# An attention and feed-forward layer: norms deferred by urgency, projections held until their rows are loaded, first norms at once, last tile in quarters

## The chip, the cores and the metric

One core of one Trainium2 chip runs the whole kernel. The time is the device time of one execution in microseconds (us). Medians are given with the number of executions behind them. A kernel's runs also carry the mean clock that was granted to TensorE (1.000 is full speed): in the runs quoted here the mean clock of one kernel differs from run to run by a few thousandths, and the time with it (the kernel before, on one chip: 918.45 us at 0.996, 917.06 at 0.998, 916.01 at 1.000). Profiled spans are some 1.7 us shorter than the times of the same executions; spans are compared with spans, and times with times.

## The reference, cut to what matters

```python
h   = x + attention(layernorm(x)) @ wo            # S=2048, D=1024, bf16
out = h + (silu(layernorm(h) @ w1) * (layernorm(h) @ w3)) @ w2   # F=3584
# attention: 32 heads of 32; 4 segments of 512 rows, one after the other.
# In a segment: softmax attention inside the segment, plus phi(q) @ M / (phi(q) @ z)
# from a memory M, z summed over earlier segments, mixed by sigmoid(beta).
```

## The kernel before

The program does not write instructions in order. It builds a graph of operations. Each has an engine, an estimated duration and a class (a lower class is more urgent), and a list scheduler fixes, at build time, the order of each engine and the semaphore waits. So a changed class or dependence moves instructions everywhere, and a dependence added to the graph is a wait in the finished kernel only where the order does not satisfy it anyway.

The kernel lets its matmuls write to one PSUM tensor of 128x4096 fp32, which its code counts as eight banks of 128x512. While attention runs, four hold scores, bank 4 and bank 5 numerators and denominators, and only banks 6 and 7 are free for all dense matmuls. A dense group (the eight matmuls of one accumulation, and the operation that evacuates the bank) takes one of the two. It is `safe`: its first matmul also takes over the write-after-read dependences of its later operations, so that a group doesn't occupy a bank and then wait.

```python
    # Graph.op: every operation joins the graph here
            if group.safe and group.ops:
                head = group.ops[0]
                for d, raw in list(o.deps.items()):
                    if not raw and d.seq < head.seq:
                        self.dep(head, d, raw=False)
# ... cut ...
    def dense_group(self, late=False):
        g = Group([(6,), (7,)],
                  ("att", [(4,), (5,), (0,), (1,), (2,), (3,)]) if late else None, True)
        return g
# ... cut ...
    def ln(self, k, src, dst, cls):               # statistics at cls - 1, L716 and L718
        # ... cut ...
        self.dve_op(lambda e: e.tensor_scalar(dst, src, mean, rs, op0=ALU.subtract,
                                              op1=ALU.mult), 540.0, [src, mean, rs], [dst], cls,
                    port=True)                    # the norm itself, L725
# ... cut ...
    def wo_stage(self, s):                        # output projection of segment s
        oT = self.oT[s % 2]
        for i in range(4):
            t = 4 * s + i
            h, hn = self.h[t % 3], self.hn[0]     # 3 buffers of rows, 1 of normed rows
            self.g.dma(h[:, :], self.x2d[t * 128:(t + 1) * 128, :], cls=2)
            for half in range(2):
                gr = self.dense_group(s >= 2)
                self.mms(gr, [(lambda gr: self.bank(gr), oT[:, c, i * 128:(i + 1) * 128],
                               self.wo[:, c, half * 512:(half + 1) * 512], c == 0, c == 7, 512)
                              for c in range(8)], 5 if s < 2 else 7)
                hs = h[:, half * 512:(half + 1) * 512]
                self.g.op("dve", dve_ns(512), lambda e, gr, hs=hs: [e.tensor_tensor(
                    hs, hs, self.bank(gr), op=ALU.add)], reads=[hs], writes=[hs], cls=1,
                    group=gr)                     # the residual add, L993
            self.g.dma(self.hd[t * 128:(t + 1) * 128, :], h[:, :], cls=3)
            self.ln(16 + t, h[:, :], hn[:, :], 4)
            self.g.dma_t(self.hnT[s][:, :, i * 128:(i + 1) * 128], hn[:, :], 2)
```

The residual add reads rows `h` that a DMA loads. That dependence is a true read-after-write one, so the safe group doesn't pass it to its first matmul: the group may take its bank before its rows are there.

The softmax here doesn't subtract the row's maximum and nothing guards it: scores larger than these inputs give would overflow.

Of the kernel before, what the change touches and what calls it, by code (L numbers as in the profile page):

```python
# [8 lines left out]
ALU = mybir.AluOpType  # L9
# [60 lines left out]
class Graph:  # L70
# [90 lines left out]
    def op(self, engs, cost, emit, reads=(), writes=(), cls=5, deps=(), group=None,  # L161
           kind=None, gate=None, port=False):
        if isinstance(engs, str):
            engs = (engs,)
        if not isinstance(cost, dict):
            cost = {e: cost for e in engs}
        o = Op(engs, cost, emit, cls, len(self.ops))
        o.kind = kind
        o.gate = gate
        o.port = port  # L170
        if gate is not None:
            self.phase_left[gate] = self.phase_left.get(gate, 0) + 1
        for ap in reads:
            self._touch(o, ap, False)
        for ap in writes:
            self._touch(o, ap, True)
        for d in deps:
            self.dep(o, d)
        o.group = group
        for group in (group.parts if isinstance(group, Both) else (group,) if group else ()):  # L180
            for prev in group.ops:
                if prev.engs != o.engs or o.engs != ("pe",):
                    self.dep(o, prev)
            if group.ops and o.engs == ("pe",):
                self.dep(o, group.ops[-1])
            o.first = not group.ops
            if group.safe and group.ops:
                head = group.ops[0]
                for d, raw in list(o.deps.items()):
                    if not raw and d.seq < head.seq:  # L190
                        self.dep(head, d, raw=False)
            group.ops.append(o)
            group.open += 1
        self.ops.append(o)
        return o
# [259 lines left out]
def act_ns(n, ptr=0):  # L455
    return 185.0 + n * 0.834 + 93.0 * ptr


def dve_ns(n, mode=1):
    return 150.0 + n / (0.96 * mode)  # L460
# [10 lines left out]
class Kernel:  # L471
# [219 lines left out]
    def ln_act(self, k, src, dst):  # L691

        sm, nm, sq = (self.lnst[:, k, i:i + 1] for i in range(3))
        junk = self.oT[0][:, 0:2, :].rearrange("p a b -> p (a b)")
        G = self.g
        G.op("act", act_ns(1024), lambda e, gr: [e.activation(junk, src, AF.Copy, accum_out=sm)],
             reads=[src], writes=[junk, sm], cls=1)
        self.act(nm, sm, AF.Copy, 190.0, cls=1, scale=-1.0 / 1024)
        G.op("act", act_ns(1024, 1), lambda e, gr: [e.activation(
            junk, src, AF.Square, bias=nm, accum_out=sq)], reads=[src, nm], writes=[junk, sq],  # L700
            cls=1)
        ve, rs = self.lnve[:, k:k + 1], self.rstd[:, k:k + 1]
        mh = self.mhalf[:, :]
        self.pool_op(lambda e: e.tensor_scalar(ve, sq, 1.0 / 1024, self.EPS, op0=ALU.mult,
                                               op1=ALU.add), 1, [sq], [ve], 0)
        self.pool_op(lambda e: e.tensor_tensor(rs, ve, mh, op=ALU.pow), 190, [ve, mh], [rs], 0)
        self.dve_op(lambda e: e.tensor_scalar(dst, src, nm, rs, op0=ALU.add, op1=ALU.mult),
                    540.0, [src, nm, rs], [dst], 2, port=True)

    def ln(self, k, src, dst, cls):  # L710

        st = self.lnst[:, k, :]
        mv = self.lnmv[:, k, :]
        for c in range(2):
            a, b = self.lnst[:, k, 6 * c:6 * c + 6], src[:, c * 512:(c + 1) * 512]
            self.dve_op(lambda e, a=a, b=b: e.bn_stats(a, b), 630.0, [b], [a], cls - 1)  # L716
        st2 = self.lnst[:, k, :].rearrange("p (a b) -> p a b", a=2)
        self.dve_op(lambda e: e.bn_aggr(mv, st2), 200.0, [st2], [mv], cls - 1)  # L718
        ve, rs = self.lnve[:, k:k + 1], self.rstd[:, k:k + 1]
        var, mean = self.lnmv[:, k, 1:2], self.lnmv[:, k, 0:1]  # L720
        mh = self.mhalf[:, :]
        self.pool_op(lambda e: e.tensor_scalar(ve, var, self.EPS, None, op0=ALU.add), 1,
                     [var], [ve], 0)
        self.pool_op(lambda e: e.tensor_tensor(rs, ve, mh, op=ALU.pow), 190, [ve, mh], [rs], 0)
        self.dve_op(lambda e: e.tensor_scalar(dst, src, mean, rs, op0=ALU.subtract,  # L725
                                              op1=ALU.mult), 540.0, [src, mean, rs], [dst], cls,
                    port=True)

    def ln1(self, s):
        for i in range(4):  # L730
            t = 4 * s + i
            x = self.xs[t % 4][:, :]
            self.g.dma(x, self.x2d[t * 128:(t + 1) * 128, :], cls=0 if s == 0 else 2)
            if t == 1:
                self.ln_act(t, x, x)
            else:
                self.ln(t, x, x, 2 if s == 0 else 5)
            if s:
                self.g.dma_t(self.xnT[s][:, :, i * 128:(i + 1) * 128], x, 3)
                continue  # L740
            gr = Group([(6,), (7,), (4,), (5,)], safe=True)
            self.transposes(gr, [(c * 128, self.xs[t % 4][:, c * 128:(c + 1) * 128])
                                 for c in range(8)], 2 if s == 0 else 4)
            out = self.xnT[s][:, :, i * 128:(i + 1) * 128]
            self.evac(gr, out, 1024, lambda b: b.rearrange("p (k n) -> p k n", k=8), cls=1,
                      bf=True)
# [234 lines left out]
    def wo_stage(self, s):  # L981
# [3 lines that stand above are left out]
            h, hn = self.h[t % 3], self.hn[0]  # L985
# [8 lines that stand above are left out]
                    hs, hs, self.bank(gr), op=ALU.add)], reads=[hs], writes=[hs], cls=1,  # L994
                    group=gr)
            self.g.dma(self.hd[t * 128:(t + 1) * 128, :], h[:, :], cls=3)
            self.ln(16 + t, h[:, :], hn[:, :], 4)
            self.g.dma_t(self.hnT[s][:, :, i * 128:(i + 1) * 128], hn[:, :], 2)

    def ffn_up(self, blk, ch):  # L1000
# [30 lines left out]
    def ffn_down(self, blk):  # L1031
        if blk == 0:
            for i in range(7):
                self.g.dma(self.w2[i][:, :, :], self.B_w2[i * 512:(i + 1) * 512, :].rearrange(
                    "(j p) n -> p j n", p=128), cls=5)
        for i in range(8):
            t = 8 * blk + i
            hr = self.hr[t % 3]
            self.g.dma(hr[:, :], self.hd[t * 128:(t + 1) * 128, :], cls=3)
            for half in range(2):  # L1040
                gr = self.dense_group(True)
                self.mms(gr, [(lambda gr: self.bank(gr), self.hm[fc][:, i * 128:(i + 1) * 128],
                               self.w2[fc // 4][:, fc % 4, half * 512:(half + 1) * 512],
                               fc == 0, fc == 27, 512) for fc in range(28)], 8,
                         eager=True)
                ob = self.ob[self.n_ob % 8][:, :]
                self.n_ob += 1
                hs = hr[:, half * 512:(half + 1) * 512]
                self.g.op("dve", dve_ns(512), lambda e, gr, hs=hs, ob=ob: [e.tensor_tensor(  # L1049
                    ob, hs, self.bank(gr), op=ALU.add)], reads=[hs], writes=[ob], cls=1,  # L1050
                    group=gr)
                self.g.dma(self.out2d[t * 128:(t + 1) * 128, half * 512:(half + 1) * 512], ob,
                           cls=1)

    def run(self):
        self.ps = self.es.enter_context(self.nc.psum_tensor("ps", [128, 4096], F32))
# [83 lines left out]
```

## Time and profile before

| | before |
|---|---|
| time, median of 4 runs beside the changed kernel | 917.87 us (916.94 to 918.2) |
| profiled span | 916.2 us, mean clock 0.996 |
| TensorE | 99% busy |
| TensorE idle in the first 332 us | 9.3 us |
| TensorE idle from 332 us to the last matmul | 0 |
| half clock | 6.83 us, from 150.9 us |

The prediction shows the lines of this profile that carry its argument. One view is added here, TensorE's waits: what it waited for, the total in us, how often, and the longest one.

```profile
PE ps L610 <- DVE xs L725: 2.4, 1, 2.4
PE ps L871 <- ACT et L884: 2.0, 5, 0.8
PE ps L598 <- DVE R0b L970: 1.5, 1, 1.5
...
PE ps L598 <- DVE h L993: 0.9, 3, 0.6
```

The first is the wait for the first norm at start-up. The third and part of the second and fourth are one place, at 148 to 152 us, which the prediction takes apart. L598 is the line of every dense matmul, L610 of the transposes, L871 of the scores, L939 of attention's numerators and denominators, L884 of the exponential. The products with the memory are `pq,zsel` and `pq,Mbf`; the second needs bank 4. 128\*128, 32\*128 and 128\*32 are the tiling modes, as the profile prints them with each matmul. A change of mode has no line of its own. The 0.10 us that the prediction gives it is an estimate from this trace: eight dense matmuls start 0.216 us apart from 25.95 us on, a score group in another mode starts at 27.77 and the next dense matmul at 28.10, so a group of some 0.21 us takes 0.33.

The trace's record of the granted clock changes at 4.17, 150.94, 157.77 and 915.53 us, the last time to half after the last matmul. From the first change these are 43, 45 and 267 times 3.413 us. A stretch of 3.41 us between two such multiples is called a window below. In the two windows at half clock, dense matmuls that follow each other start 0.427 us apart, as from 155.03 to 157.16, and at full clock 0.216.

### The profile page before, as it was taken

To read this page: it belongs to the slowest core of one execution; us is meant where nothing else is said; L and a number is where in the kernel's file an instruction comes from. 1 tells how busy PE (TensorE), PEld (TensorE's weight loads), DVE (VectorE), ACT (ScalarE), POOL (GpSimd) and SP (SyncE) were. 2 spreads that over 40 slices of the span, in tenths; PEclk is the share of its full clock that TensorE was granted. 3 is DMA by queue.
4 is the path that set the end of the run, shared out by engine and by line. 5 is a ranking of instruction groups with operands and counts; after the bars stand their busy time and mean duration, and the time that the engine had idled before them with its cause. 6 is when DMAs were issued, how large, how long until landed. Compare 5 with 4: busy or idle time off the path is not lost.

```text
span 916.2 us, 12998 instructions
## 1 busy us (share of the span) xinstructions
PE 904.0 (99%) x5472; PEld 404.1 (44%) x5472; DVE 432.8 (47%) x735; ACT 297.7 (32%) x316; POOL 176.2 (19%) x274
## 2 busy tenths in 40 slices
PE   8999998999999999999999999999999999999998
PEld 5444443444444444444444444444444444444443
DVE  3867877877856764634634311211343334331111
ACT  5878865877677611111111100000111111110000
POOL 2545655456553420100100000000000000000000
PEclk9999998999999999999999999999999999999999
DMA  9957655443531355833733121012133212301110
GB/s 311 248 166 214 156 138 116 127 126 112 141 119 41 90 207 158 187 101 93 174 102 92 47 70 47 14 38 80 53 98 92 64 52 69 93 24 40 35 41 29
DMA packets 145241, 96.26 MB, mean 105 GB/s; under 512 B 45344, under 2 KB 132384, under 8 KB 145184
## 3 DMA queue, kind: packets, MB, share of 16 engines
q1 hardware_dynamic: 145184, 95.45, 37.9%
q8 instruction: 43, 0.70, 0.3%
q14 instruction: 14, 0.11, 0.1%
HBM read 76.55 MB, written 8.39 MB: 93 GB/s over the span
## 4 chain that ended last, share of the span: by engine, by line
PE 96%; ACT 1%; DVE 1%; DMA 0%; issue 0%; SPq 0%; DVEq 0%
PE ps L598 89%; PE ps L939 4%; PE ps L871 3%; ACT et L884 1%; DMA xs<-in_A_x_dram 0%; DVE lnst L716 0%; PE ps L610 0%; DVE h L993 0%; DVE hn L725 0%; SPq L203 0%; DVE T L950 0%; DVE R0b L965 0%; DVE R0b L970 0%; DVE qT L622 0%; DVE xnT L622 0%
## 5 line engine op out<-in xcount | busy, mean ns | idle before, releaser
L598 PE MATMUL ps<-hnT,w1b 128*128 128x512 bf16 x896 | 223.2, 379 | 0.0
L598 PE MATMUL ps<-hnT,w3b 128*128 128x512 bf16 x896 | 222.3, 379 | 0.0
L1019 ACT ACTIVATE sg<-ps 128x512 bf16<-128x512 f32 x112 | 66.9, 597 | 442.6 <-PE ps L598 439.9
L598 PE MATMUL ps<-w2b,hm 128*128 128x512 bf16 x896 | 196.3, 379 | 0.0
L1022 DVE SCALAR_TENSOR_TENSOR t<-sg,ps 128x512 bf16<-128x512 bf16 x112 | 76.9, 687 | 210.6 <-ACT sg L1019 210.6
L884 ACT ACTIVATE et<-ps 128x2048 bf16<-128x2048 f32 x80 | 149.9, 1874 | 34.2 <-PE ps L871 17.9
L598 PEld LDWEIGHTS ps<-w2b,hm 128*128 128x128 bf16 x896 | 87.7, 98 | 105.7
L598 PEld LDWEIGHTS ps<-hnT,w3b 128*128 128x128 bf16 x896 | 87.3, 98 | 106.0 <-issue 1.2
L598 PEld LDWEIGHTS ps<-hnT,w1b 128*128 128x128 bf16 x896 | 87.0, 98 | 106.3 <-issue 6.4
L889 POOL TENSOR_SCALAR_AFFINE_SELECT et<-et 128x512 bf16<-128x512 bf16 x128 | 88.7, 710 | 118.6 <-ACT et L884 118.3
L1027 DVE SCALAR_TENSOR_TENSOR hm<-t,ps 128x512 bf16<-128x512 bf16 x112 | 76.9, 687 | 37.6 <-PE ps L598 34.5
L1049 DVE TENSOR_TENSOR ob<-hr,ps 128x512 bf16<-128x512 bf16 x32 | 22.0, 687 | 143.4 <-PE ps L598 143.4
L598 PE MATMUL ps<-hnT,wp 128*128 128x512 bf16 x256 | 63.5, 390 | 0.9 <-DVE h L993 0.6
L598 PE MATMUL ps<-xnT,wp 128*128 128x512 bf16 (+1 forms) x288 | 60.2, 356 | 0.3 <-DVE xnT L622 0.3
L598 PE MATMUL ps<-wo,oT 128*128 128x512 bf16 x256 | 59.5, 380 | 0.3 <-DVE h L993 0.3
L950 DVE STREAM_TRANSPOSE T<-ps 128x512 f32<-128x512 f32 x32 | 22.9, 717 | 37.4 <-PE ps L939 37.3
L598 PEld LDWEIGHTS ps<-xnT,wp 128*128 128x128 bf16 x288 | 26.5, 98 | 27.1 <-issue 4.2
L598 PEld LDWEIGHTS ps<-hnT,wp 128*128 128x128 bf16 x256 | 23.7, 100 | 31.8 <-issue 7.2
L598 PEld LDWEIGHTS ps<-wo,oT 128*128 128x128 bf16 x256 | 24.0, 98 | 30.7 <-issue 2.2
L976 POOL TENSOR_TENSOR Nm<-Nm,R1b 128x512 f32<-128x512 f32 x24 | 30.4, 1268 | 32.6 <-DVE R1b L965 32.5
L871 PE MATMUL ps<-qT,kT 32*128 32x128 bf16 (+3 forms) x512 | 31.9, 302 | 2.2 <-ACT et L884 2.0
L598 PE MATMUL ps<-wp,hnT 128*128 128x512 bf16 x128 | 30.8, 380 | 0.0
(85 smaller groups left out, 592.6 us busy)
## 6 DMA issues: line engine op xcount, KB each, us to landing
w1b<-in_B_w_dram SPq DMA_DIRECT2D x28, 512.0 KB, 3.9
w3b<-in_B_w_dram SPq DMA_DIRECT2D x28, 512.0 KB, 4.7
wp<-in_A_wk_dram SPq DMA_DIRECT2D x8, 1024.0 KB, 5.6
wp<-in_A_wv_dram SPq DMA_DIRECT2D x8, 1024.0 KB, 5.3
wp<-in_A_wq_dram SPq DMA_DIRECT2D x7, 1024.0 KB, 5.7
w2b<-in_B_w_dram SPq DMA_DIRECT2D x7, 1024.0 KB, 8.6
xs<-in_A_x_dram SPq DMA_DIRECT2D x16, 256.0 KB, 5.8
h<-in_A_x_dram SPq DMA_DIRECT2D x16, 256.0 KB, 3.3
```

The source lines that it names most:

```text
L598: return [e.matmul(p[0](gr), p[1], p[2], start=p[3], stop=p[4]) for p in part]
L871: ins.append(e.matmul(self.bank(gr, j, 512 - 128 * kc, off), k[r, g, 128 * kc:128 * kc + 128], q[r, g, 128 * kc:512], start=True, stop=Tru ...
L884: return [e.activation(et[:, :, :], src, AF.Exp, scale=self.scale)]
L889: self.pool_op(lambda e, m=m: e.affine_select(m, m, pattern=[[0, 4], [1, 128]], compare_op=ALU.is_ge, fill=0.0, base=0, channel_multiplier ...
L939: ins.append(e.matmul(self.ps[r, b * 512 + 128 * kc:(b + 1) * 512], lhsT, pieces[kc][:, j, :], start=kc == 0 and (what == "n" or s == 0), ...
L950: G.op("dve", dve_ns(512), lambda e, gr: [e.transpose(T1, self.bank(gr))], writes=[T1], cls=0, group=gd)
L976: self.either(lambda e: e.tensor_tensor(Nm, Nm, R1, op=ALU.mult), 512, 2, [Nm, R1], [Nm], 2)
L1019: self.g.op("act", act_ns(512), lambda e, gr, sg=sg: [e.activation(sg, self.bank(gr), AF.Tanh, scale=0.5)], writes=[sg], cls=2, group=gg)
L1022: e.scalar_tensor_tensor(t1, sg, 1.0, self.bank(gr), op0=ALU.add, op1=ALU.mult)], reads=[sg], writes=[t1], cls=2,
L1027: e.scalar_tensor_tensor(dst, t1, 0.5, self.bank(gr), op0=ALU.mult, op1=ALU.mult)], reads=[t1], writes=[dst], cls=2,
L1049: self.g.op("dve", dve_ns(512), lambda e, gr, hs=hs, ob=ob: [e.tensor_tensor(ob, hs, self.bank(gr), op=ALU.add)], reads=[hs], writes=[ob], ...
```

## The change

Four edits, all of the order; apart from the last tile, which is cut differently, no instruction is added or removed by hand.

1. **Hold**: the first matmul of a dense group also takes over a dependence on a load, so a projection claims its bank only when its rows are there.
2. **Deferral**: the norms after the projection go from class 4 to 6, those of later segments from 5 to 5, 6 and 7, so that evacuations go ahead of them.
3. **First norms at once**: the norms of the first four tiles get class 0.
4. **Quarters**: the last output tile is computed in columns of 512, 256 and 256, so that the last evacuation and store are half as large.

```diff
-                    if not raw and d.seq < head.seq:
-                        self.dep(head, d, raw=False)
+                    if (not raw or d.kind == "dma") and d.seq < head.seq:
+                        self.dep(head, d, raw=raw)
@@ ln_act, the norm itself
-                    540.0, [src, nm, rs], [dst], 2, port=True)
+                    540.0, [src, nm, rs], [dst], 0, port=True)
@@ ln, the norm itself
-                                              op1=ALU.mult), 540.0, [src, mean, rs], [dst], cls,
-                    port=True)
+                                              op1=ALU.mult), 540.0, [src, mean, rs], [dst],
+                    0 if k < 4 else cls, port=True)
@@ ln1
-                self.ln(t, x, x, 2 if s == 0 else 5)
+                self.ln(t, x, x, 2 if s == 0 else 4 + s)
@@ wo_stage
-            self.ln(16 + t, h[:, :], hn[:, :], 4)
+            self.ln(16 + t, h[:, :], hn[:, :], 6)
@@ ffn_down
-            for half in range(2):
+            cols = [(0, 512), (512, 256), (768, 256)] if t == 15 else [(0, 512), (512, 512)]
+            for c0, n in cols:
                 gr = self.dense_group(True)
     ... cut: matmuls, add and store of columns c0 to c0 + n in place of half * 512 to ... + 512
```

More of the change, by code (lines that the diff above doesn't have):

```diff
@@ L1039, in ffn_down @@
             self.g.dma(hr[:, :], self.hd[t * 128:(t + 1) * 128, :], cls=3)
-            for half in range(2):
+            cols = [(0, 512), (512, 256), (768, 256)] if t == 15 else [(0, 512), (512, 512)]
+            for c0, n in cols:
                 gr = self.dense_group(True)
-                self.mms(gr, [(lambda gr: self.bank(gr), self.hm[fc][:, i * 128:(i + 1) * 128],
-                               self.w2[fc // 4][:, fc % 4, half * 512:(half + 1) * 512],
-                               fc == 0, fc == 27, 512) for fc in range(28)], 8,
-                         eager=True)
-                ob = self.ob[self.n_ob % 8][:, :]
+                self.mms(gr, [(lambda gr, n=n: self.bank(gr, 0, n),
+                               self.hm[fc][:, i * 128:(i + 1) * 128],
+                               self.w2[fc // 4][:, fc % 4, c0:c0 + n],
+                               fc == 0, fc == 27, n) for fc in range(28)], 8, eager=True)
+                ob = self.ob[self.n_ob % 8][:, 0:n]
                 self.n_ob += 1
-                hs = hr[:, half * 512:(half + 1) * 512]
-                self.g.op("dve", dve_ns(512), lambda e, gr, hs=hs, ob=ob: [e.tensor_tensor(
-                    ob, hs, self.bank(gr), op=ALU.add)], reads=[hs], writes=[ob], cls=1,
+                hs = hr[:, c0:c0 + n]
+                self.g.op("dve", dve_ns(n), lambda e, gr, hs=hs, ob=ob, n=n: [e.tensor_tensor(
+                    ob, hs, self.bank(gr, 0, n), op=ALU.add)], reads=[hs], writes=[ob], cls=1,
                     group=gr)
-                self.g.dma(self.out2d[t * 128:(t + 1) * 128, half * 512:(half + 1) * 512], ob,
-                           cls=1)
+                self.g.dma(self.out2d[t * 128:(t + 1) * 128, c0:c0 + n], ob, cls=1)
     def run(self):
```

## The prediction

> **What bounds the kernel now.** I read four views in this order: the page's busy shares, busy time by stretch, TensorE's order of time around each place where it waits, and the order of time of all engines at the worst of them. First the page and the stretches.
>
> ```profile
> PE 904.0 (99%) x5472; PEld 404.1 (44%) x5472; DVE 432.8 (47%) x735; ACT 297.7 (32%) x316; POOL 176.2 (19%) x274
> ...
> 0.00:332.00 332.00, 322.69 (x2780) 0.99 0.54 148
> 332.00:913.20 581.20, 581.20 (x2696) 1.00 0.29 81
> 913.20:916.20 3.00, 0.08 (x1) 0.89 0.13 44
> ```
>
> The reader is to see that TensorE is the bound and that most of the span is closed to this change. From 332 us on, 2696 matmuls take 581.2 us, 0.2156 us each, with no idle time: that is the feed-forward part, already a solid stream. Everything that a new order can win lies in the first 332 us (9.3 us shown idle, plus any slow clock) and in the 3 us after the last matmul. Two per cent would be 18.4 us, more than all of that together. So the answer "within 2%" is nearly settled before the change is read.
>
> Then the one bad place, in TensorE's order of time:
>
> ```profile
> 146.89 1.04 PE L598 MATMUL ps<-wo,oT 128*128 128x512 bf16 x4
> 147.79 0.39 PE L598 MATMUL ps<-pq,zsel 128*128 128x512 bf16 x1
> 148.94 0.40 PE L871 MATMUL ps<-qT,kT 32*128 32x256 bf16 x8 [0.77 <-ACT et L884]
> 150.81 0.52 PE L598 MATMUL ps<-pq,Mbf 128*128 128x512 bf16 x1 [1.47 <-DVE R0b L970]
> 151.32 0.61 PE L871 MATMUL ps<-qT,kT 32*128 32x512 bf16 x4
> ...
> 152.50 1.86 PE L598 MATMUL ps<-hnT,wp 128*128 128x512 bf16 x4 [0.56 <-DVE h L993]
> 154.16 1.07 PE L598 MATMUL ps<-v,pkn 128*128 128x129 bf16 x8
> 155.03 3.25 PE L598 MATMUL ps<-hnT,wp 128*128 128x512 bf16 x8
> ```
>
> Three waits in a row with nothing between them, then eight dense matmuls that take 3.25 us where eight others take 1.90. The stretches say why:
>
> ```profile
> 147.50:150.90 3.40, 1.16 (x12) 1.00 0.69 179
> 150.90:157.80 6.90, 6.34 (x24) 0.51 0.57 132
> 157.80:164.70 6.90, 6.90 (x65) 1.00 0.30 66
> ```
>
> TensorE was busy a third of 3.4 us, and then its granted clock (the column after the count) was half for 6.9 us. Why it was idle is in the order of time of the other engines:
>
> ```profile
> 146.74 0.58 SPq L203 DMA_DIRECT2D h<-in_A_x_dram x1
> ...
> 150.68 1.08 DVE L725 TENSOR_SCALAR hn<-h,lnmv,rstd 128x1024 bf16<-128x1024 bf16 x1
> ...
> 151.68 1.27 DVE L993 TENSOR_TENSOR h<-h,ps 128x512 bf16<-128x512 bf16 x2
> ```
>
> Both halves of one output projection were done by 147.7 us and held the only two banks that dense work may use, because their residual add (L993) needs rows whose load was issued only at 146.74, and stood behind a norm (L725) that the load itself had waited behind. With both banks held there was no dense matmul to put between attention's dependent steps.
>
> [...] the record of the granted clock has one drop, from 150.9 us for 6.83 us[...]. [...]
>
> **Part 1, projections held until their rows are loaded.** The first matmul of a projection group now takes over the load dependence of its evacuation, so it claims a bank only when the add can follow at once. The static order of the changed kernel (both orders can be listed without a run) shows the effect: in this section the dense matmuls of the next segment's q and k stand where the pair of banks was blocked, and the fourth projection tile moves some 50 dense matmuls later. Value: from 147.79 to 152.50 are 4.71 us. The work in them is two dense matmuls (0.43), two score groups (0.43) and four changes of tiling mode. A change costs about 0.10 (28.09 - 27.77 for a score group of 0.21). Together 1.26, so 3.45 us were lost. From 152.50 to 158.21 are 5.71 us for 12 dense matmuls (2.59), 8 of 129 columns (0.45) and one change (0.1), so 2.57 us were lost to the clock. **Sum: -6.0 us**, all on the path, as TensorE is the path.
>
> **Part 2, norms deferred.** No instruction is added or removed. Projection norms fall from class 4 to 6 and those of later segments to 5, 6 and 7, below evacuations. What it is worth is read from TensorE's other waits, all small. For each bank-4 chain I count the work that the order puts between attention's column matmuls and the memory product that needs the bank; VectorE's chain takes some 3.85 us (146.96 to 150.81). Before, one of the 24 places falls clearly short (1.5 us of work); after, one falls short by little (3.2). For each pair of score groups I count the work between; ScalarE's exponential (1.88 us and its hand-over) needs about 2.05. A place with eight dense matmuls (1.83) loses 0.2, as seen at 142.12. Before, apart from the bad place: two such, one of 0.9 at 224 to 226, one of 0.2 at 45, some 1.3 us. After: three of 0.2, one of 0.8 and one of 0.85, some 2.25 us. The first wait, at 34 to 36 us, is the same in both orders. Against it, waits for a bank at 99.7 (0.5) and 216 (0.35) should shrink when evacuations go ahead of norms; I grant 0.4. **Sum: +0.6 us.** Changes of tiling mode go from 206 to 209 by the orders: **+0.3 us.**
>
> **Part 3, first norms at once.** Now the first transposes wait for L725 until 8.71. After, the first norm goes ahead of three statistics: ready when its rstd is (6.28), so its transposes start near 7.0, 1.7 us earlier. But TensorE then waits again. The second norm follows at 8.4 (was 8.69), and the third and fourth come no earlier, since statistics moved behind the first: about 9.6 and 10.9 against 9.26 and 10.51. The first projection needs the second tile's copy, which now follows the first on ScalarE and ends near 10.55 (the matmul started at 10.74). The solid stream starts at 12.06 before and about 11.95 after. **Sum: -0.1 us**: the early start becomes an idle gap in the middle.
>
> **Part 4, last tile in a half and two quarters.** The last add takes 0.69 us for 512 columns; an add of 258 columns (Macc, L833) takes 0.41, so -0.27. The last matmul of 256 columns ends 0.1 sooner after its start (273 ns against 379 for 512). 56 matmuls of 256 columns at 0.109 us (the start-to-start time of the first projection's) cost 6.10 us instead of 28 at 0.2156, 6.04: +0.06. The final store is half as large, but its 2.2 us from issue to end look like fixed latency. **Sum: -0.3 us.**
>
> **Total:** -6.0 + 0.6 + 0.3 - 0.1 - 0.3 = -5.5, so 917.6 becomes **912.1 us**.
>
> **The rivals.** (a) A wait in place of the one removed: the held projections come later and load something else, or the deferred norms make a transposed input late. For it: VectorE is 80% busy from 50 to 250 us[...], with weight loads now standing behind transposes of deferred norms. Against it: TensorE waited for no DMA anywhere before, and the feed-forward's inputs are ready tens of us ahead in the new order. It would cost 1 to 4 us: 913 to 916. (b) A clock drop elsewhere. At start-up the matmuls now come in three short bursts with gaps of 1.4 and 0.6 us; a window from 7.6 to 11.0 would be less than half busy. Before, a window with a third busy dropped the clock, one with about half did not. A drop there costs 1.7 to 3.4 us, and would hide half of the gain: 914 to 915.5. (c) The bad place is no loss of its own, and what is saved there is lost to ScalarE's pace later: the span would be 916 to 918. Against it: ScalarE is busy 0.7 of the attention part only. (d) More gain: small waits vanish too, as deferral intends; of the 9 to 10 us lost up to 332 us, 8 would return: 909.5.
>
> **Range and chances.** The centre is the sum; (d) sets the lower end, 909.5, and (a) or (b) the upper, 915.5. Runs of one kernel spread 1.3 us, well inside. Faster by over 2% needs 899.3, more than all idle time, 1%. Slower by over 2% needs 18 us of new waits with the same instructions, 1%. Within 2%: 98%.
>
> **What would show it right or wrong.** Right: granted clock full in all slices; no wait of TensorE over 1 us after start-up; no L993 wait with both banks held; idle time up to 332 us near 6.5 instead of 9.3; first transposes near 7 us with the stream still starting near 12; last add 0.4 us. Wrong: half clock at start-up or near a new wait; TensorE waiting for a DMA; a stream that starts before 11 us (then part 3 was worth over a microsecond); or a bad place that stays, which would mean that the held bank was not its cause.

## The result, and the profile after

| | before | after |
|---|---|---|
| median | 917.87 us (4 runs) | 913.88 us (4 runs, 913.11 to 914.47) |
| ratio, with its 95% interval | | 0.9958 (0.9940 to 0.9975) |
| profiled span | 916.2 us at clock 0.996 | 911.4 us at clock 1.000 |
| TensorE idle in the first 332 us | 9.3 us | 6.5 us |
| last matmul's start to the end | 3.32 us | 2.84 us |

A ratio is the mean time of one kernel's fast runs over that of the other's of the same rounds, so it is not quite the ratio of the medians. The gain is 4.0 us by the medians and 4.8 us by the profiled spans; 5.5 were predicted, and 913.88 lies in the range of 909.5 to 915.5.

The page's row for TensorE, then busy time by stretch (from and to, length, TensorE's busy time with its matmuls, granted clock, DMA share, GB/s):

```profile
PE 902.3 (99%) x5500; PEld 406.1 (45%) x5500; DVE 434.3 (48%) x744; ACT 293.7 (32%) x310; POOL 175.0 (19%) x272
...
0.00:332.00 332.00, 325.50 (x2801) 1.00 0.57 152
332.00:908.50 576.50, 576.50 (x2700) 1.00 0.28 79
908.50:911.40 2.90, 0.32 (x3) 1.00 0.16 45
```

The feed-forward stream is untouched. The first 332 us hold 2801 matmuls where they held 2780, with 2.8 us less of idle time and no slow clock.

The former bad place, in TensorE's order of time, and the two stretches that had shown it:

```profile
147.29 0.40 PE L871 MATMUL ps<-qT,kT 32*128 32x256 bf16 x8
147.62 0.39 PE L598 MATMUL ps<-pq,zsel 128*128 128x512 bf16 x1
147.85 2.75 PE L598 MATMUL ps<-hnT,wp 128*128 128x512 bf16 x12
150.53 0.39 PE L871 MATMUL ps<-qT,kT 32*128 32x512 bf16 x4
...
147.50:150.90 3.40, 3.40 (x26) 1.00 0.00 0
150.90:157.80 6.90, 6.90 (x63) 1.00 0.35 108
```

Between one set of scores and the next there are now 12 dense matmuls where there was only a product with the memory. In the second stretch TensorE does 63 matmuls where it did 24.

TensorE's waits after:

```profile
PE ps L871 <- ACT et L884: 1.7, 5, 0.8
...
PE ps L598 <- DVE qT L622: 0.7, 2, 0.3
...
PE ps L598 <- DVE R0b L970: 0.2, 1, 0.2
```

The waits for L993 are gone, and of the 1.5 us for L970 there is left one of 0.2, at 298 us. The start-up's wait of 2.4 us has become two, 1.1 and 0.6. In the order of time at start-up this is, before:

```profile
8.71 1.77 PE L610 MATMUL ps<-ident,xs 128*128 128x128 bf16 x24 [2.42 <-DVE xs L725]
...
12.06 1.15 PE L598 MATMUL ps<-xnT,wp 128*128 128x256 bf16 x9
```

and after:

```profile
7.48 0.61 PE L610 MATMUL ps<-ident,xs 128*128 128x128 bf16 x8
9.23 0.61 PE L610 MATMUL ps<-ident,xs 128*128 128x128 bf16 x8 [1.14 <-ACT xnT L621]
10.46 0.62 PE L610 MATMUL ps<-ident,xs 128*128 128x128 bf16 x8 [0.62 <-DVE xs L725]
...
12.36 0.82 PE L598 MATMUL ps<-xnT,wp 128*128 128x256 bf16 x6
```

The first transposes start 1.2 us earlier, and the solid stream starts no earlier. At the other end, VectorE's last add, before and after:

```profile
913.32 0.69 DVE L1049 TENSOR_TENSOR ob<-hr,ps 128x512 bf16<-128x512 bf16 x1 [3.56 <-PE ps L598]
```

```profile
908.86 0.42 DVE L1050 TENSOR_TENSOR ob<-hr,ps 128x256 bf16<-128x256 bf16 x1 [0.89 <-PE ps L598]
```

Where the 4.8 us of the spans came from can be read from four marks in TensorE's order. The stream starts 0.30 later. The last column matmul of attention starts at 329.83 in place of 331.77, with 12 more dense matmuls (2.59 us) already done: taking off the 0.30, the middle gained 4.83. From there to the last matmul's start there is 0.2 more (0.07 of it for the quarters: 56 matmuls 0.109 us apart in place of 28 at 0.216). The tail after the last matmul's start gained 0.48. The sum is +0.30 - 4.83 + 0.2 - 0.48 = -4.8.

### The profile page after: what moved, and what is told of

Its sections match the earlier page's. It is cut to its first block, busy times and chain, and to the rows that moved or that the text cites. A ratio compares the mean times of both kernels' runs of the same rounds, so it can differ in the third digit from the quotient of the medians.

```text
span 911.4 us, 13038 instructions
## 1 busy us (share of the span) xinstructions
PE 902.3 (99%) x5500; PEld 406.1 (45%) x5500; DVE 434.3 (48%) x744; ACT 293.7 (32%) x310; POOL 175.0 (19%) x272
## 4 chain that ended last, share of the span: by engine, by line
PE 97%; ACT 2%; DVE 1%; DMA 0%; issue 0%; SPq 0%
PE ps L598 90%; PE ps L939 4%; PE ps L871 3%; ACT et L884 1%; DMA xs<-in_A_x_dram 0%; DVE lnst L716 0%; DVE qT L622 0%; PE ps L610 0%; DVE xs L725 0%; SPq L203 0%; ACT v L621 0%; ACT qT L621 0%; DVE ob L1050 0%; DVE xs L707 0%; DVE lnmv L718 0%
## 5 line engine op out<-in xcount | busy, mean ns | idle before, releaser
L598 PE MATMUL ps<-w2b,hm 128*128 128x512 bf16 (+1 forms) x924 | 196.4, 373 | 0.0
L598 PEld LDWEIGHTS ps<-w2b,hm 128*128 128x128 bf16 x924 | 90.4, 98 | 103.3
L1050 DVE TENSOR_TENSOR ob<-hr,ps 128x512 bf16<-128x512 bf16 (+1 forms) x33 | 22.1, 671 | 143.1 <-PE ps L598 143.1
```

The source lines that it names most:

```text
L598: return [e.matmul(p[0](gr), p[1], p[2], start=p[3], stop=p[4]) for p in part]
L1050: self.g.op("dve", dve_ns(n), lambda e, gr, hs=hs, ob=ob, n=n: [e.tensor_tensor(ob, hs, self.bank(gr, 0, n), op=ALU.add)], reads=[hs], wri ...
```

## The experiments

**Theory A** is the prediction's: the hold is what gains, because a projection that waits for its rows with both banks held leaves TensorE nothing to do; the other parts are worth some tenths. **Rival B**: it is the deferral, or the first norms, or any reshuffling of the order, and the hold merely goes along. **Rival C**: the gain is the clock drop alone. Twelve runs were made, on two chips: ten other kernels, and the changed kernel twice more. All were correct. Medians below are beside those of the kernel before on the same chip: 917.29 us on the first (9 runs; six at clock 0.998 with 916.82 to 917.42, three at 0.996 with 918.11 to 919.5), and 917.29 and 917.28 on the second.

### One part alone, or one undone

**e1_hold_only** is the kernel before with the hold line alone.

```diff
-                    if not raw and d.seq < head.seq:
-                        self.dep(head, d, raw=False)
+                    if (not raw or d.kind == "dma") and d.seq < head.seq:
+                        self.dep(head, d, raw=raw)
```

> Only the new dependence of a projection group on its load, all else as before. Theory (a held bank emptied TensorE's queue of dense work): the three waits from 147.8 to 152.5 us and the half clock after them are gone, 911.9 to 913.5 us. Rival (the gain comes from the norms' deferral): 917 to 918 us with the clock drop still there.

Measured: 914.73 us (914.41 to 914.95, clock 1.000 in all runs), ratio 0.9967 (0.9954 to 0.9981). The drop of the clock is gone, and 2.6 us are gained, or 1.3 against the single run of before at full clock (916.01 us, on the other chip). The 911.9 to 913.5 expected was missed: the hold doesn't gain all that the bad place lost, because the new order has waits elsewhere, one of 0.85 us for an L993 at 155.7 and two of 1.0 and 0.8 between score groups at 225 and 237.

**e2_no_hold** is the changed kernel with the hold undone: deferral, first norms and quarters stay.

```diff
-                    if (not raw or d.kind == "dma") and d.seq < head.seq:
-                        self.dep(head, d, raw=raw)
+                    if not raw and d.seq < head.seq:
+                        self.dep(head, d, raw=False)
```

> The changed kernel without that dependence, with the norms deferred. Its instruction order has a place near 155 us where only 0.6 us of work stands between attention's column matmuls and the memory product that needs bank 4. Theory: two to four us of waits in a row there, perhaps with a clock drop, 915.5 to 918.5 us. Rival (deferral alone brings the gain): within 0.5 us of the changed kernel, 913.4 to 914.4.

Measured: 927.44 us (927.01 to 928.38, clock 0.989 to 0.991), ratio 1.0108 (1.0093 to 1.0124). That is far outside the 915.5 to 918.5 expected: the direction was right, the size was not. It is slower than the kernel before by 10 us, and slower than the changed kernel (912.87 on the same chip) by 14.6. TensorE, the queue and VectorE at its worst place, and the stretch of slow clock:

```profile
153.17 0.73 PE L939 MATMUL ps<-et,v 128*32 128x512 bf16 x16 [2.71 <-ACT Nm L921]
155.71 0.61 PE L598 MATMUL ps<-pq,zsel 128*128 128x512 bf16 x1 [0.82 <-DVE T L950]
...
151.12 1.48 DVE L725 TENSOR_SCALAR hn<-h,lnmv,rstd 128x1024 bf16<-128x1024 bf16 x1
153.91 0.58 SPq L203 DMA_DIRECT2D h<-in_A_x_dram  x1
158.15 1.27 DVE L993 TENSOR_TENSOR h<-h,ps 128x512 bf16<-128x512 bf16 x2
...
153.90:164.10 10.20, 7.95 (x38) 0.50 0.48 109
```

The deferred norm L725 reads rows from a buffer that the next load overwrites; it ends at 152.6, the load is issued at 153.91, and the adds L993 that free the banks end past 159. From 149.8 to 158.9 us no matmul of a projection runs, and attention's steps wait one after the other (2.71, 0.82, 0.55 and 0.81 us). The clock is at half for 10.2 us here, and for 6.8 more at 242.6, where the same happens to the second segment's last projection tile. So the deferral by itself makes the bad place worse, and the hold is what makes the deferral possible.

**e3_first_only** is the kernel before with class 0 for the first norms alone.

```diff
-                    540.0, [src, nm, rs], [dst], 2, port=True)
+                    540.0, [src, nm, rs], [dst], 0, port=True)
-                                              op1=ALU.mult), 540.0, [src, mean, rs], [dst], cls,
-                    port=True)
+                                              op1=ALU.mult), 540.0, [src, mean, rs], [dst],
+                    0 if k < 4 else cls, port=True)
```

> Only the first norms at once. At start-up it should gain nothing: the solid stream starts between 12.0 and 12.5 us, as in the changed kernel. But its instruction order, shuffled by this small edit alone, no longer has the empty place of the kernel before. Theory (the loss sits in the order of instructions and not in the start): 911.8 to 914 us although the start is no better. Rival (the empty place needs the hold to vanish): 917 to 918.5 us.

Measured: 913.67 us (913.5 to 914.28, clock 1.000), ratio 0.9957 (0.9944 to 0.9971). This edit at 7 us gains 3.6 us, more than the hold alone. Not at start-up: its stream starts at 11.92, 0.14 earlier. The gain is at the bad place:

```profile
149.76 0.39 PE L598 MATMUL ps<-pq,Mbf 128*128 128x512 bf16 x1
150.94 0.81 PE L598 MATMUL ps<-hnT,wp 128*128 128x512 bf16 x3 [0.79 <-DVE h L993]
...
150.11 1.29 DVE L993 TENSOR_TENSOR h<-h,ps 128x512 bf16<-128x512 bf16 x2 [0.38 <-DMA h<-in_A_x_dram]
```

The add still waits for its load (0.38 us), and TensorE for the add. But the scheduler, started off differently, has put the projection later: the last weight loads of its two halves are at 146.5 and 148.7 us in place of 144.0 and 147.3, and the second half fills the place between two sets of scores (147.4 to 149.3). The load is issued at the same time as before (146.72) and lands at 150.1 in place of 150.8. So both banks are held at once for 2.1 us in place of 5.0, TensorE waits 0.8 us in place of three waits of 2.8 us in all, and the clock stays up.

**e4_after_again** is the changed kernel unaltered, on the same chip as e1 to e3.

> The changed kernel again, to see why two of its four runs took 1.3 us longer, at a mean clock of 0.998 instead of 1.0. Theory: in some runs one window of 3.4 us falls into the start-up, between 7 and 15 us, at half clock; if the profiled run is one of these (912.7 us span), its clock record shows it there. Rival: the drop falls later, at the waits near 244 us (0.8 us) or 298 us.

Measured: 912.87 us (912.82 to 913.35, five runs, clock 1.000 in all), ratio 0.9949 (0.9937 to 0.9962), 4.4 us below before. No run showed the clock of 0.998, so the question that it was made for stayed open.

**e5_no_first** is the changed kernel with the classes of the first norms put back, on the second chip, where **e12_after_third**, the changed kernel unaltered once more, stands beside it.

```diff
-                    540.0, [src, nm, rs], [dst], 0, port=True)
+                    540.0, [src, nm, rs], [dst], 2, port=True)
-                    0 if k < 4 else cls, port=True)
+                    cls, port=True)
```

> The changed kernel without its start-up part (first norms in their old order). My estimate for that part was a gain of 0.1 us. Theory (nothing is gained, as the fourth norm sets when the stream of matmuls starts): within 0.7 us of the changed kernel, 912.3 to 914.3 us. Rival (the profile of the changed kernel shows a stream that starts 0.3 us later, so the part costs something): faster than the changed kernel by 0.5 us or more. Its instruction order has two short places between score groups fewer (0.2 us each), which would go the same way.

> The changed kernel beside these on the same chip, 912.8 to 913.4 us at clock 1.0; about a quarter of its runs so far were at 0.998 and near 914.4. If the profiled run is one, its clock record should show the half clock between 7 and 15 us.

Measured: e5 912.87 us (912.59 to 913.14), e12 913.17 us (912.86 to 913.27); every run at clock 1.000. With the other parts there, the first norms are worth nothing that these runs can show. Given e3, this is the plainest sign that the parts do not add up.

**e6_no_defer** is the changed kernel with classes 4 and 5 of the deferred norms put back.

```diff
-                self.ln(t, x, x, 2 if s == 0 else 4 + s)
+                self.ln(t, x, x, 2 if s == 0 else 5)
-            self.ln(16 + t, h[:, :], hn[:, :], 6)
+            self.ln(16 + t, h[:, :], hn[:, :], 4)
```

> The changed kernel without the deferral of the norms: hold, first norms and quarters only. Theory (deferral is worth little once projections are held): 912.5 to 914.5 us, the changed kernel's time within 1 us. Rival (deferral is what puts evacuations in time): 916 us or more. The instruction order shows five places of 1.2 to 1.6 us of work between score groups, some 3 us of waits, so I lean to 914.

Measured: median 916.3 us, ratio 0.998 (0.9967 to 0.9992). The median fits the rival, but the clock makes it so. Its runs fall in two sets: 914.54 and 914.75 at clock 1.000, and 916.30, 916.32 and 916.42 at 0.998. The profile fell on one of the latter and shows the half clock at start-up, from 10.9 to 14.3 us. At full clock the deferral is therefore worth about 914.6 - 913.2 = 1.4 us once the hold is there, where the prediction had put it at a loss of 0.6.

**e7_tail_only** is the kernel before with the last tile in quarters (the loop over `cols` in the diff above).

```diff
-            for half in range(2):
+            cols = [(0, 512), (512, 256), (768, 256)] if t == 15 else [(0, 512), (512, 512)]
+            for c0, n in cols:
```

> Only the last tile in a half and two quarters. The instruction order is the same as before up to there. Expected: 0.3 to 0.5 us less than before in the span of runs with the same mean clock (the time from the last matmul's start to the end falls from 3.3 to 2.8 us in the changed kernel's profile). Rival: the two more stores cost as much as the shorter add saves, no change.

Measured: 917.71 us (916.76 to 919.26), ratio 1.0004 (0.9991 to 1.0016): inconclusive, for the clock's scatter (0.994 to 0.998 in its own runs) moves the time by more than the 0.3 sought. At clock 0.998 the two runs have a mean of 917.0, against 917.2 for before. What the run did show is the scatter itself. Before's profile had half clock for two windows, and this one, with the same bad place, for one:

```profile
152.80:156.20 3.40, 3.40 (x16) 0.50 0.80 193
156.20:159.60 3.40, 3.24 (x42) 1.00 0.78 187
```

In the kernel before, the first window at half clock (150.9 to 154.3) had TensorE busy for 2.85 us and was followed by another; here TensorE is busy throughout. That fits the groups of times of the kernel before: at clock 0.996, two slow windows, as its profile shows; at 0.998, one. The groups' means are 918.6 and 917.1 on the first chip and 918.1 and 917.2 on the second, so by these differences a window costs an estimated 0.8 to 1.5 us. One run of before had clock 1.000 and took 916.01 us.

### The cause by another route: rows early

If theory A is right about the mechanism, the hold itself isn't needed: rows that are loaded early enough do the same. **e8_more_row_buffers** is the kernel before with five row buffers instead of three (two borrowed from the input tiles), and no hold, no deferral, nothing else.

```diff
-            h, hn = self.h[t % 3], self.hn[0]
+            h, hn = (self.h + self.xs[2:4])[t % 5], self.hn[0]
```

> The kernel before with five buffers for residual rows instead of three (two idle buffers of the first norms are lent), so that the fourth tile's rows are loaded long before they are added; no hold, no deferral. Theory (banks were held because rows came late): the waits and the clock drop at 150 us are gone without any hold, 911.5 to 914 us. Rival (the norm ahead of the residual add on VectorE, not the load, kept the banks): 916.5 us or more.

Measured: 912.04 us (911.47 to 912.12 at clock 1.000, one run of 913.25 at 0.998), ratio 0.9938 (0.9925 to 0.9952). This one line gives more than the whole change. The fourth tile's load (into a lent `xs` buffer) is issued at 119.61 us in place of 146.74, its add waits for TensorE's own last matmul, and TensorE has no wait in its former bad place:

```profile
119.61 0.34 SPq L203 DMA_DIRECT2D xs<-in_A_x_dram  x1
...
147.04 0.69 DVE L993 TENSOR_TENSOR xs<-xs,ps 128x512 bf16<-128x512 bf16 x1 [0.87 <-PE ps L598]
...
151.31 0.40 PE L871 MATMUL ps<-qT,kT 32*128 32x256 bf16 x8
151.63 2.76 PE L598 MATMUL ps<-hnT,wp 128*128 128x512 bf16 x12
```

Adding the hold to this kernel, in the version with quarters below, changes no engine's order when both are listed: with the rows there, it has nothing to hold. By itself e8 doesn't settle the cause, for its edit also reorders every engine, as e3's does. What settles it is a time that all the traces hold, for how long both halves of one projection stood finished with neither add done (from the last weight load of the second to the end of the first one's add, at most, in attention):

| kernels | both banks held, us | time |
|---|---|---|
| e2 | 9.6, and 7.5 at the second place | 927.4 |
| before, e7 | 5.0 | 917.3, 917.7 |
| e3 | 2.1 | 913.7 |
| e9 | 1.6 | 915.9 |
| all others, the changed kernel among them | 0.1 to 0.9 | 911.5 to 916.3 |

In the profiles every drop of the clock between start-up and the last matmul is in a kernel of the first two rows (10.2 and 6.8 us in e2, 6.83 in before, 3.4 in e7; the other profiled runs have a mean clock of 1.000, or of 0.998 in e6 and e8, with the drop at start-up), and each edit that removes the bad place shortens this time, by whatever way. So the held pair of banks is the cause of the bad place. It is not the cause of all differences: e1 and e9, for instance, lose to waits between score groups. Rival C, the clock alone, has against it the one run of before at full clock: 916.01 us is still 2.8 above e12, so of the 4.1 us between those two kernels on this chip the waits make the larger part.

**e9_deferral_more_buffers** is e2 (deferral, first norms and quarters without the hold, the slowest kernel) with the same line.

```diff
-            h, hn = self.h[t % 3], self.hn[0]
+            h, hn = (self.h + self.xs[2:4])[t % 5], self.hn[0]
```

> The slow kernel of the second experiment (deferral, first norms, quarters, no hold: 927.4 us) with five buffers for residual rows instead of three. Built with the hold and without it, this kernel has the same instruction order on every engine, so with rows loaded early the hold has nothing left to do. Theory (deferral hurts only by delaying the row loads behind the norms, and the hold is the cure for that alone): 911.5 to 913.5 us. Rival (deferral hurts by itself, for instance through VectorE's order): 918 us or more.

Measured: 915.85 us (915.47 to 916.17 at clock 1.000, 917.47 at 0.998), ratio 0.9984 (0.9971 to 0.9996). Early rows recover 11.6 of the 14.6 us that the missing hold costs (e2 and e9 ran on different chips; before is the same on both). The expectation of 911.5 to 913.5 failed all the same. Three places between score groups hold only 0.96 us of other work, and each then waits 1.02 us for the exponential:

```profile
202.13 0.40 PE L871 MATMUL ps<-qT,kT 32*128 32x512 bf16 x4 [1.02 <-ACT et L884]
```

(the others are at 221.8 and 231.4). They stood in the order of instructions before the run, and I had not counted them. With the hold added to this kernel the order of every engine is the same, so they are no cost of a missing hold.

**e10_buffers_and_quarters** is e8 with the last tile in quarters.

```diff
-            h, hn = self.h[t % 3], self.hn[0]
+            h, hn = (self.h + self.xs[2:4])[t % 5], self.hn[0]
... and the loop over cols as in e7
```

> The kernel before with five row buffers and the last tile in a half and two quarters: the version with the fewest short places in its instruction order. The buffers alone gave 911.9 us in runs at clock 1.0, the quarters should take 0.4: 911.2 to 911.8 us at clock 1.0 and 1.3 to 1.8 more in a run with one half-clock window at the start-up. Rival: the quarters give nothing here, 911.9.

Measured: 911.51 us (911.17 to 911.98, all at clock 1.000), ratio 0.9934 (0.9920 to 0.9947). It is the fastest version found, 5.8 us below before and 1.7 below the changed kernel on the same chip. Against e8 at full clock it gains about 0.4, as large as the 0.48 in the two first traces, but hardly more than the scatter of either.

### The clock at start-up

The record of the clock begins with a change to full clock, at 4.2 us in before and 6.9 in after; until then the warm-up matmuls start about 0.43 us apart and after it about 0.22, so a mean clock of 1.000 leaves this start out. In e8's profile it falls at 5.7. The later changes lie 43, 45 and 267 times 3.413 us after it in before, and the one in after 265 times.

e8's profile caught the slow clock of the prediction's rival (b). From its change to full clock, by stretch:

```profile
5.70:9.10 3.40, 1.35 (x6) 1.00 1.13 313
9.10:12.50 3.40, 3.23 (x27) 0.50 1.07 337
```

A stretch with 1.35 of 3.40 us busy is followed by one at half clock. In e6 it was 1.60 of 3.40. In the changed kernel's profile the stretch from 6.9 to 10.3 has 1.79 busy and no drop follows; before had 2.10 and 2.03 in its first two and none. The cost, from runs with and without it, is 1.4 us in e8 and 1.7 in e6, at or below the low end of the 1.7 to 3.4 that the prediction gave (an estimate, which fits half of 3.4 and of 6.83 us).

With the drops in attention, the views of these runs show this. Half clock came after stretches of 3.4 us with TensorE busy for 1.08 (e7), 1.16 (before), 1.35 (e8) and 1.60 us (e6); in e2 the 3.8 us before its two drops had 1.09 and 1.31. It went on after a window with 2.85 busy (before, from 150.94) and ended after windows with 3.41 (before), 3.40 (e6, e7) and 3.23 (e8). Busy time is the view's, with modelled ends, and the cases are few: these are readings, from which no limit follows, and that busy time is what decides was not shown.

**e11_longer_warm_up** is e10 with 24 in place of 16 matmuls in the warm-up that runs before the first norms are ready.

```diff
-        self.mms(gr, [(lambda gr: self.bank(gr), wl, w, True, True, 512)] * 16, 0, split=16)
+        self.mms(gr, [(lambda gr: self.bank(gr), wl, w, True, True, 512)] * 24, 0, split=24)
```

> The same with 24 warm-up matmuls instead of 16; no other instruction moves. Theory (a start-up window in which TensorE is busy for about a third of 3.4 us is followed by half clock): the eight more fill the wait before the first transposes, no run shows a mean clock of 0.998 any more, all within 911.1 to 912.0 us. Rival: the eight delay the first transposes[...], up to 1 us more in every run.

Measured: 911.79 us (911.66 to 912.34, all at clock 1.000), ratio 0.9938 (0.9925 to 0.9952). No run had the drop, but e10 had none either, so whether a longer warm-up prevents it stays open; one run, at 912.34, missed the 912.0 expected. It seems not to be free: the first transposes start at 9.18 in place of 8.41 and the stream at 12.52 in place of 12.14 (one profile each; three profiles of the changed kernel have 12.36 to 12.60).

## Why the prediction was right, point by point

- **"Within 2%", and the stream from 332 us.** Right: all idle time and slow clock together came to an estimated 16 us (9.3 idle, 3.4 as half of the 6.83 us at half clock, 3.0 at the end), and the ratio is 0.9958. The stream stayed solid (576.50 of 576.50 us).
- **The bad place and its cause.** Right, and shown by two independent edits: e1 (hold) and e8 (rows early) both remove it, and e2 makes it worse by making the rows later. In one reading the prediction took two norms for one, since both are L725: the load waited behind the norm of 144.59, the add behind that of 150.68. The rows landed at 150.79 and the add began at 151.68, so the norm cost 0.9 us and the late rows the rest. The waits, the L993 wait and the half clock at 150 us are gone in the changed kernel, and the idle time to 332 us is 6.5 us, as predicted.
- **Its size, "-6.0 us".** The middle gained 4.8 where -6.0 + 0.6 + 0.3 = -5.1 had been worked out, so for the profiled pair the sum of the middle was good. But the clock term in it, 2.57 us, is that of a run with two slow windows, as the profile happened to be; a run with one loses 0.8 to 1.5 less. The difference between 4.8 by the spans and 4.0 by the medians comes from the runs after, two of which had clock 0.998: their median is 0.8 above the profiled run.
- **The assignment of the 6.0 us to the hold.** This step did not hold as put. The hold alone gains 2.6 us (e1), the first norms alone 3.6 (e3), and given all else the hold is worth 14.6 (e2 against e4) and the first norms nothing (e5 against e12). What stood in one column of the sum as "the hold's" is what any edit gains that keeps both banks from being held at once. Step by step on the one path on record, from 917.3: the hold -2.6 (e1), first norms and quarters -0.1 (e6 at full clock), deferral -1.4 (e12). So the total came near partly by luck, through two errors of opposite sign: the hold was put too high and the deferral on the wrong side.
- **Deferral, "+0.6 us".** Partly wrong. Counting the work between score groups was good: between the two groups at 242.9 and 245.3 us TensorE is idle for 0.75 us against the 0.8 predicted, between those at 297.6 and 299.9 for 0.57 against 0.85, and at three places it waits 0.15 against 0.2. The 0.4 granted for bank waits at 99.7 and 216 did not come as such: those waits are gone, but after has new ones of 0.33, 0.33 and 0.18 at 46, 74 and 107 us. And against the kernel that has the hold and not the deferral (e6), deferral is worth -1.4 us at equal clock. The prediction had compared with the kernel before, which is not the same question.
- **First norms, "-0.1 us" at start-up.** The mechanism was right: the first transposes came earlier (7.48 for "near 7.0") and the stream did not. Its start, 12.36, is 0.3 later than before; over the profiles of these kernels without a slow window it lies between 11.8 and 12.6, so the difference isn't the edit's alone.
- **Quarters, "-0.3 us".** Right: 0.48 in the trace after the last matmul's start, less some 0.1 for the 56 matmuls; in times it is too small to resolve alone (e7). The final store was expected to take as long at half the size: from its issue to the end are 2.18 us before (914.03 to 916.21, 128 KB) and 2.08 after (909.31 to 911.39, 64 KB).
- **Rival (b), a slow window at start-up.** It is real in e6 and e8, where a profile caught it (half clock from 10.9 and from 9.1 us). The stretch that the prediction calls about half busy had 2.03 of 3.40 us. In the changed kernel two of the first four runs have clock 0.998 and are 1.2 us above the other two on average (914.4 against 913.2), which would fit it; none of the nine later runs had it, and no profile caught one. That it is the start-up there is inferred, not shown.
- **Rivals (a), (c), (d).** TensorE still waits for no DMA, against (a). The saved time wasn't lost again to ScalarE, against (c): the span is 911.4 and not 916. Of (d) little came: the small waits moved more than they vanished.

## What to carry to other kernels

Let a matmul group claim a PSUM bank only when everything that its evacuation needs is there, or, better where memory allows, load those inputs early: two more row buffers gave here more than four edits of the order (912.0 us alone and 911.5 with the quarters, against 912.9 to 913.2), and made the hold idle. Under a scheduler that fixes the order at build time, the parts of the change did not add (the hold gained 2.6 us alone and 14.6 given the rest): judge a version by the work that its order puts between dependent steps, and ask what an edit is worth given the others, not alone. Where the differences are below a per cent, compare runs of equal mean clock: the kernel before took 916.01 to 918.45 us on one chip, at clocks from 1.000 to 0.996.
